# Spreading three batches' transform stages over a gated FFN, with a first stage in three products

## The chip, the cores and the metric

The kernel runs on one core of a Trainium2 chip. The metric is the device time of one execution in microseconds (us), the median of several runs. Engines are named as in the profile: PE (TensorE matmul), PEld (its weight loads), DVE (VectorE), ACT (ScalarE), POOL (GpSimd), SP (SyncE, which here issues nearly all DMAs, in order).

## The reference

For `x` of 8 batches x 3136 positions x 256 channels: a real FFT along the positions, a product with a complex filter, the inverse FFT, and then a gated feed-forward network whose gate is a three-tap convolution along the positions:

```
X = rfft(x, axis=1);  y = irfft(X * (filt_r + 1j * filt_i), n=3136, axis=1)
h = maximum(y @ w_in, 0)                       # 256 -> 1024
conv[s] = sum_k conv_w[k] * h[s + k - 1]       # per channel, zeros outside the batch
out = (h * sigmoid(conv)) @ w_out              # 1024 -> 256
```

## The kernel before, in words

**The transform of a batch** is four stages of matmuls, each in 14 operations of two columns ("pairs", q = 0 to 13). 3136 = 112 x 28. Stage "1" multiplies 112 rows of x by a table of its own for every column (`s1`), stage "2" does the 28-point transforms, then DVE multiplies by the filter in three instructions and POOL adds (`filt`), stage "3" goes back, and stage "4" multiplies by another table for every column (`m2`) and leaves y, which is kept in SBUF as two fp32r parts, a rounded one and the rest. Between "1" and "2", and between "3" and "4", the data go through DRAM (`a_dram`, `r_dram`, `b_dram`), because rows and columns change places. So "2" of a batch can load only when its "1" is stored completely, and "4" when its "3" is (`ready`).

A float32 matmul costs PE more than an fp32r one. Where accuracy asks for it, `mm3` replaces one float32 product by three fp32r products of parts (rounded x rounded, rounded x rest, rest x rounded). The FFN's matmuls (lines 187 to 189 under the name `ps_h`, and 586 to 588) are of this kind, and so is stage "2" from batch 2 on: stage "1" stores both parts (`store_first`). Stages "1" (line 275), "3" (line 279) and "4" (line 313) are plain float32.

**The FFN** runs in units of 510 positions, each with 8 blocks of 128 hidden channels. One unit and block is one *step* m; there are 400. A step's work is pipelined over seven steps: `inner(m)` (the matmuls into `ps_h`, 3 PSUM banks), then relu and the taps on ACT and DVE, sigmoid, gate, the split into `g` parts (ACT rounds, POOL subtracts), and six steps later `project`, which adds to `po`. At the last block of a unit (every step with m = 6 modulo 8), DVE copies `po` out (`evacuate`, line 599) and SP stores it (lines 604 and 617).

**The order around the change** is written out by hand, and every engine and SP keep it. Batch 0's transform runs ahead of the loop. From then on the transforms of batches 1 to 7 are placed into steps: `plan[m]` lists the operations of step m. With NW = 48 steps a batch, window t holds stages "2", "3" and "4" of batch t and stage "1" of batch t + 1: "2" at steps 2 to 25 of the window (9 steps for 5 operations), "3" three steps behind it, "4" at steps 33 to 44 (more than one a step), and "1" in the steps with least other work. In each step come, in this order: `evacuate`; `from_bank` for the operations of the step before (PSUM bank `ps_t` to SBUF, stores); `want_in` (loads); `transform` for the new operations, at the head of PE's step; `inner`; the FFN's other parts; `project`.

`want_in` loads the inputs in the order of the plan, at most 6 ahead. It stops at the first one whose stage is not stored yet, or whose buffers are all out: three `tia` for stage "2" (two loads each, line 244), three `tin` for "1" and "4" (line 253). `want_table` loads the tables of "1" and "4" (line 678; three operations ahead, four `tab` buffers), `want_filter` the filter of the next "2" (line 683, two buffers). PSUM has three `ps_t` banks.

Where a unit reaches into the next batch, `join_tail` and `join_head` copy the tail of one y and the head of the next into a tile `yx`.

Of the kernel before, what the change touches and what calls it, by code (L numbers as in the profile page):

```python
# [17 lines left out]
N1 = 112  # L18
# [18 lines left out]
def _dft_tables():  # L37
# [78 lines left out]
    tall[:N1] = s1  # L116
    return {"s1": tall, "s2": s2(False), "s2s": s2(True), "one": np.eye(128), "s3": s3(False), "s3s": s3(True), "m2": m2, "m2g": turned}

# [14 lines left out]
def tile_fft_filter_gated_ffn(  # L133
# [7 lines left out]
    w_out: bass.AP,  # L141
    s1: bass.AP,
    s2: bass.AP,
    s2s: bass.AP,
# [67 lines left out]
    wo = [wc.tile([128, NF, D], F32R, name=f"wo{h}") for h in range(2)]  # L212
    turned = [wc.tile([120, 2, D], F32, name=f"v{k}") for k in range(2)]
    for v in turned:
# [21 lines left out]
    def load_in(pool, kind, b, q):  # L236
        if kind == "2" and b == 1:
            r = pool.tile([112, 2, 2, D], F32R, name="tia", bufs=3)[:, 0].bitcast(F32)
            nc.sync.dma_start(out=r, in_=a_in[b][:, pair(q)])
            return r  # L240
        if kind == "2":
            r = pool.tile([112, 2, 2, D], F32R, name="tia", bufs=3)
            for h, t in enumerate((a_in, r_in)):
                nc.sync.dma_start(out=r[:, h].bitcast(F32), in_=t[b][:, pair(q)])
            return r
        if kind == "1" and b == 1:
            if q % 2 == 0:
                t = pool.tile([128, 2, 2, D], F32, name="filt")
                nc.sync.dma_start(out=t.rearrange("p a j d -> p (a j) d"), in_=xt[N1:N1 + 128, 2 * q:2 * q + 4])
                fours.append(t)  # L250
            return fours[-1][0:112, q % 2]
        r = pool.tile([128, 2, D], F32, name="tin", bufs=3)[0:112]
        nc.sync.dma_start(out=r, in_={"1": xv, "4": b_in}[kind][b][:, pair(q)])
        return r
# [18 lines left out]
    def by_column(ps, w, r):  # L273
        for j in range(2):
            nc.tensor.matmul(ps[0:112, j * D:j * D + D], lhsT=w[:, j], rhs=r[:, j], start=True, stop=True)  # L275

    def by_row(o, q, r, m, ms):
# [20 lines left out]
    def filt(ps, q, f):  # L298

        pp, v = ps[0:120].rearrange("p (j d) -> p j d", d=D), turned[q % 2]  # L300
        z = tp.tile([128, 2, D], F32, name="z", bufs=3)[0:120]
        nc.vector.tensor_mul(z, pp, f[0:120, :, 0])
        nc.vector.tensor_mul(v[64:120], pp[0:56], f[0:56, :, 1])
        nc.vector.scalar_tensor_tensor(out=v[0:56], in0=pp[64:120], scalar=-1.0, in1=f[64:120, :, 1], op0=ALU.mult, op1=ALU.mult)  # L304
        nc.gpsimd.tensor_tensor(out=z, in0=z, in1=v, op=ALU.add)  # L305
        return z
# [13 lines left out]
    raws = {}  # L320
    conv_raw = tp.tile([128, 1, 6 * NF], I32, name="conv_raw", bufs=1)

    def load_weights(k, pool):
        if pool is tp:
            raws[k] = [pool.tile([128, 2, 2, D], F32R, name="tia", bufs=3).rearrange("p a j d -> p a (j d)").bitcast(I32) for _ in range(2)]
# [14 lines left out]
    def convert(k, pool):  # L340

        for j in range(2):
            if pool is tp:
                if j == 0:
                    em = pool.tile([128, 2, 2, D], F32R, name="tia", bufs=3).bitcast(I32)
                w, raw = pool.tile([128, 2, D], F32, name="z", bufs=3), raws[k][j]
# [14 lines left out]
    with (  # L361
# [39 lines left out]
        with tc.tile_pool(name="sq", bufs=2) as sq:  # L401
# [43 lines left out]
            for i in range(NP + 4):  # L445
# [18 lines left out]
                if i == 5:  # L464
                    table("1", 0)
                    for q in range(AHEAD):
                        r = tp.tile([128, 2, D], F32, name="tin", bufs=3)
                        nc.sync.dma_start(out=r, in_=xt[N1:N1 + 128, pair(q)])
# [8 lines left out]
        for q in range(NP + 1):  # L477
# [3 lines left out]
            if q:  # L481
# [141 lines left out]
    def put(m, kind, b, q):  # L623
        plan.setdefault(m, []).append((kind, b, q))

    for t in range(1, B):
        w = NW * (t - 1)
        used = [0] * NW
        if t == 1:
            at1 = [q // 2 for q in range(NP - AHEAD)]  # L630
            at2, at4 = [9 + 3 * q // 2 for q in range(NP)], [35 + 10 * q // NP for q in range(NP)]
            for q, s in enumerate(at1):
                put(s, "1", 1, AHEAD + q)
                used[s] += 1
        else:
            at2, at4 = [2 + 9 * q // 5 for q in range(NP)], [33 + 12 * q // NP for q in range(NP)]
        for q in range(NP):
            for s, kind, cost in ((at2[q], "2", 3), (at2[q] + 3, "3", 1), (at4[q], "4", 1)):
                put(w + s, kind, t, q)
                used[s] += cost  # L640
        if t + 1 < B:
            spots = []
            for q in range(NP):
                s = min(range(5 if t == 1 else 0, NW - 2), key=lambda s: (used[s], s))
                used[s] += 2
                spots.append(s)
            for q, s in enumerate(sorted(spots)):
                put(w + s, "1", t + 1, q)
        tails[w + 29] = heads[w + 46] = next(u for u in range(NU) if joins(u) and place(u)[0] == t - 1)
        assert NF * tails[w + 29] >= w + NW  # L650
    order = [(m, op) for m in sorted(plan) for op in plan[m]]
    inputs = [op for _, op in order if op[0] in "124"]
    tables = [op for _, op in order if op[0] in "14"]
    filters = [op for _, op in order if op[0] == "2"]
# [4 lines left out]
    def ready(op):  # L659
        kind, b, _ = op  # L660
        return kind == "1" or stored.get(({"2": "1", "4": "3"}[kind], b), 0) == NP

# [11 lines left out]
    def want_table(n):  # L674
        for op in tables[n:n + 1]:
            src = {"1": s1, "4": m2}[op[0]]
            got_table[op] = t = tp.tile([112, 2, 112], F32, name="tab", bufs=4)
            nc.sync.dma_start(out=t, in_=src[0:112, pair(op[2])])

# [4 lines left out]

    done, wanted = {"in": 0, "table": 0, "filter": 0}, {"in": 0}
    def transform(op):
        kind, b, q = op
        banks[op] = ps = ps_t.tile([128, 512], F32, name="ps_t")
        if kind in "124":
            done["in"] += 1  # L690
            r = got_in.pop(op)
        if kind in "14":
            want_table(done["table"] + 3)
            done["table"] += 1
            w = got_table.pop(op)
        if kind == "1":
            by_column(ps, w, r)
        if kind == "2":
# [5 lines left out]
        if kind == "4":  # L704
            fourth(ps, r, w)

    def from_bank(op):
# [11 lines left out]
        if kind == "4":  # L719
            vs[op] = v = tp.tile([128, 2, D], F32, name="z", bufs=3).rearrange("p j d -> p (j d)")[:, 0:4 * N1]  # L720
            nc.vector.tensor_copy(v, ps[:, 0:4 * N1])
# [10 lines left out]
    with tc.manual_schedule(engines=COMPUTE | {mybir.EngineType.SP}):  # L732
        want_in()
        for n in range(3):
            want_table(n)
        late = convert(3, tp)
        for m in range(NF * NU + PLAG + 1):
            p1, p2, p3, p4, p6, p7 = (at(m - k) for k in (1, 2, 3, 4, PLAG, PLAG + 1))
            new, old = plan.get(m, []), plan.get(m - 1, [])
            if p7:  # L740
# [83 lines left out]
```

## Time and profile before

| | |
|---|---|
| median of 3 runs (lowest, highest) | 1540.9 us (1539.38, 1542.57) |
| the profiled execution: time, span | 1538.35 us, 1536.5 us |
| granted TensorE clock, mean | 0.997 |
| stage "1" of batches 2 to 7: 336 instructions (four to an operation) | 86.3 us of busy time |
| DMA: bytes moved, mean rate | 268.46 MB, 175 GB/s |
| DMA queue of SP: share of 16 engines' span | 58.0% |

Rows of groups read: line, engine, operation, what it writes <- reads, shape, how often | busy us in total, mean ns of one | idle time before them and who ended it. A matmul's mean is its latency; matmuls overlap, so the cost of one to PE is the distance to the next. Rows of the timeline read: start, duration, engine, line, operation; those of the chain: start, duration, what. Rows of waits: who waited <- for whom: us in total, times, longest.

### The profile page before, as it was taken

To read this page: it belongs to the slowest core of one execution; us is meant where nothing else is said; L and a number is where in the kernel's file an instruction comes from. 1 tells how busy PE (TensorE), PEld (TensorE's weight loads), DVE (VectorE), ACT (ScalarE), POOL (GpSimd) and SP (SyncE) were. 2 spreads that over 40 slices of the span, in tenths; PEclk is the share of its full clock that TensorE was granted. 3 is DMA by queue.
4 is the path that set the end of the run, shared out by engine and by line. 5 is a ranking of instruction groups with operands and counts; after the bars stand their busy time and mean duration, and the time that the engine had idled before them with its cause. 6 is when DMAs were issued, how large, how long until landed. Compare 5 with 4: busy or idle time off the path is not lost.

```text
span 1536.5 us, 26897 instructions
## 1 busy us (share of the span) xinstructions
PE 1506.2 (98%) x9292; PEld 1305.2 (85%) x9292; DVE 1235.6 (80%) x1894; ACT 1143.7 (74%) x1973; POOL 830.8 (54%) x725
## 2 busy tenths in 40 slices
PE   6989999999999999999999999999999999999999
PEld 5867789888898889988898888988899888989998
DVE  7988886888778887788878987788877888777776
ACT  3576678766787777876788667876688667888886
POOL 4635456554574455645565455745556455754443
PEclk9999999999999999999999999999999999999999
DMA  8768764787539755597546885388554763300001
GB/s 301 246 180 241 233 202 136 222 251 210 170 117 275 233 172 179 154 268 228 176 137 203 238 241 170 109 252 256 171 173 117 207 182 99 106 29 15 28 28 31
DMA packets 188967, 268.46 MB, mean 175 GB/s; under 512 B 19056, under 2 KB 130528, under 8 KB 188832
## 3 DMA queue, kind: packets, MB, share of 16 engines
q1 hardware_dynamic: 188352, 266.29, 58.0%
q8 instruction: 74, 1.21, 0.3%
q14 instruction: 61, 0.50, 0.1%
q10 hardware_dynamic: 480, 0.46, 0.1%
HBM read 176.76 MB, written 89.92 MB: 174 GB/s over the span
## 4 chain that ended last, share of the span: by engine, by line
PE 88%; DVE 4%; issue 3%; DMA 2%; POOL 2%; ACT 1%; SPq 0%; POOLq 0%; ACTq 0%; DVEq 0%
PE ps_h L187 11%; PE ps_h L189 11%; PE ps_h L188 11%; PE po L586 11%; PE po L588 11%; PE po L587 11%; PE ps_t L313 6%; PE ps_t L279 5%; PE ps_t L275 5%; PE ps_t L187 1%; PE ps_t L188 1%; PE ps_t L189 1%; POOL g L162 1%; DMA tin<-b_dram 1%; PE ps L386 1%
## 5 line engine op out<-in xcount | busy, mean ns | idle before, releaser
L554 DVE SCALAR_TENSOR_TENSOR t<-ps_h,cw,t 128x510 f32<-128x510 f32 (+1 forms) x800 | 588.6, 736 | 247.3 <-ACT t L550 243.7
L162 POOL TENSOR_TENSOR g<-t,g 128x510 fp32r<-128x510 f32 (+1 forms) x400 | 506.2, 1275 | 200.4 <-ACT g L156 186.7
L586 PE MATMUL po<-wo,g 128*128 128x256 f32 (+1 forms) x1576 | 439.6, 279 | 0.1
L588 PE MATMUL po<-wo,g 128*128 128x256 f32 (+1 forms) x1576 | 439.1, 279 | 0.0
L587 PE MATMUL po<-wo,g 128*128 128x256 f32 (+1 forms) x1576 | 438.6, 278 | 0.0
L550 ACT ACTIVATE t<-ps_h,cw 128x510 f32<-128x510 f32 (+1 forms) x400 | 272.7, 682 | 151.4 <-POOL g L162 122.0
L545 ACT ACTIVATE ps_h<-ps_h 128x512 f32<-128x512 f32 (+1 forms) x400 | 235.2, 588 | 178.5 <-PE ps_h L189 176.1
L305 POOL TENSOR_TENSOR z<-z,v 120x512 f32<-120x512 f32 x112 | 145.5, 1299 | 356.6 <-DVE v L304 291.1
L187 PE MATMUL ps_h<-y,wi 128*128 128x512 f32 (+1 forms) x688 | 311.5, 453 | 2.9 <-DVE t L560 1.7
L586 PEld LDWEIGHTS po<-wo,g 128*128 128x128 f32 (+1 forms) x1576 | 296.7, 188 | 17.1 <-ACT g L156 0.3
L587 PEld LDWEIGHTS po<-wo,g 128*128 128x128 f32 (+1 forms) x1576 | 296.1, 188 | 17.2
L588 PEld LDWEIGHTS po<-wo,g 128*128 128x128 f32 (+1 forms) x1576 | 296.6, 188 | 0.5 <-POOL g L162 0.4
L189 PE MATMUL ps_h<-y,wi 128*128 128x512 f32 (+1 forms) x688 | 269.8, 392 | 0.3 <-POOL wi L162 0.3
L188 PE MATMUL ps_h<-y,wi 128*128 128x512 f32 (+1 forms) x688 | 269.6, 392 | 0.0
L560 DVE TENSOR_TENSOR t<-ps_h,t 128x510 f32<-128x510 f32 (+1 forms) x400 | 268.6, 672 | 1.1 <-ACT t L557 0.8
L557 ACT ACTIVATE t<-t 128x510 f32<-128x510 f32 (+1 forms) x400 | 245.5, 614 | 3.0 <-DVE t L554 2.9
L156 ACT ACTIVATE g<-t 128x510 fp32r<-128x510 f32 (+1 forms) x400 | 245.1, 613 | 0.2 <-DVE t L560 0.2
L162 POOL TENSOR_TENSOR y<-z,y 128x448 fp32r<-128x448 f32 x98 | 138.4, 1422 | 98.7 <-ACT y L156 94.8
L187 PEld LDWEIGHTS ps_h<-y,wi 128*128 128x128 f32 x688 | 129.9, 189 | 39.8 <-DVE t L560 7.8
L189 PEld LDWEIGHTS ps_h<-y,wi 128*128 128x128 f32 x688 | 129.8, 189 | 30.6 <-POOL wi L162 0.7
L188 PEld LDWEIGHTS ps_h<-y,wi 128*128 128x128 f32 x688 | 130.4, 189 | 29.8 <-issue 10.9
L313 PE MATMUL ps_t<-tab,tin 112*128 112x112 f32 x784 | 102.0, 274 | 3.9 <-DMA tin<-b_dram 2.0
(124 smaller groups left out, 1718.4 us busy)
## 6 DMA issues: line engine op xcount, KB each, us to landing
filt<-in_filt SPq DMA_DIRECT2D x98, 512.0 KB
tia<-a_dram SPq DMA_DIRECT2D x98, 224.0 KB
b_dram<-st SPq DMA_DIRECT2D x98, 224.0 KB
tin<-b_dram SPq DMA_DIRECT2D x98, 224.0 KB
a_dram<-sh SPq DMA_DIRECT2D x90, 224.0 KB
tin<-in_x SPq DMA_DIRECT2D x84, 224.0 KB
r_dram<-sh SPq DMA_DIRECT2D x84, 224.0 KB
tia<-r_dram SPq DMA_DIRECT2D x84, 224.0 KB
```

What stands on the lines that cost most here:

```text
L156: nc.scalar.activation(dst, src, AF.Copy)
L162: nc.gpsimd.tensor_tensor(out=dst, in0=src, in1=hi.bitcast(F32), op=ALU.subtract)
L187: nc.tensor.matmul(ps, lhsT=wh, rhs=rh, start=start, stop=False, **kw)
L188: nc.tensor.matmul(ps, lhsT=wh, rhs=rl, start=False, stop=False, **kw)
L189: nc.tensor.matmul(ps, lhsT=wl, rhs=rh, start=False, stop=stop, **kw)
L550: nc.scalar.activation(t, hs[u, f][:, 1:n + 1], AF.Copy, scale=cw[:, 1, f:f + 1])
L554: nc.vector.scalar_tensor_tensor(out=t, in0=h[:, k:place(u)[2] + k], scalar=cw[:, k, f:f + 1], in1=t, op0=ALU.mult, op1=ALU.add)
L557: nc.scalar.activation(ts[u, f], ts[u, f], AF.Sigmoid)
L560: nc.vector.tensor_mul(ts[u, f], hs.pop((u, f))[:, 1:place(u)[2] + 1], ts[u, f])
L586: nc.tensor.matmul(o, lhsT=gh[:, c:c + n], rhs=wo[0][:, f], start=first, stop=False, skip_group_check=True)
L587: nc.tensor.matmul(o, lhsT=gh[:, c:c + n], rhs=wo[1][:, f], start=False, stop=False, skip_group_check=True)
L588: nc.tensor.matmul(o, lhsT=gl[:, c:c + n], rhs=wo[0][:, f], start=False, stop=last, skip_group_check=True)
```

## The change

Stage "1" from batch 2 on is made of three fp32r products. Its table comes as two parts, made on the host (`s1p`) and copied by seven DMAs into a DRAM tile of its own (`s1_dram`) while batch 0's stage "4" runs; each operation loads two `tab` tiles, one for each column. The parts of x are made by POOL in a new operation "0", which stands two steps ahead of its "1": a cast and a subtraction into a tile `parts`.

The plan is new. Stages are spread by hand-given ranges (`at1`, `at2`, `at4`) over more steps, so that up to three batches are under way in one window, and `settle` moves an operation on until its step has no more than one other. The buffers change: `tia` 3 to 2, `tin` 3 to 4, `tab` 4 to 5, `z` 3 to 4, `parts` 2 new. `yx`, the late weight conversion's scratch and `conv_raw` use tiles of `parts` and `z` instead of their own, and `join_tail` moves from step 29 to step 44 of a window. In the new plan, stages "2" to "4" of batches 2 to 7 stand in these steps: "2" 50-71, 85-108, 123-150, 166-193, 207-238, 241-278; "3" three steps later; "4" 76-92, 115-140, 158-187, 201-235, 244-283, 289-330. Stage "1" stands in 10-38, 58-80, 83-119, 122-162, 165-203, 206-232.

```diff
+    parts[:, :, 0] = ((whole.view(np.uint32) + np.uint32(0x800)) & np.uint32(0xFFFFF000)).view(np.float32)
+    parts[:, :, 1] = whole - parts[:, :, 0]
...
+    s1_dram = dram.tile([N1, N2, 2, 112], F32, name="s1_dram")
...
-            r = pool.tile([112, 2, 2, D], F32R, name="tia", bufs=3)
+            r = pool.tile([112, 2, 2, D], F32R, name="tia", bufs=2)
...
-        r = pool.tile([128, 2, D], F32, name="tin", bufs=3)[0:112]
-        nc.sync.dma_start(out=r, in_={"1": xv, "4": b_in}[kind][b][:, pair(q)])
+        r = pool.tile([128, 2, D], F32, name="tin", bufs=4)[0:112]
+        nc.sync.dma_start(out=r, in_={"0": xv, "4": b_in}[kind][b][:, pair(q)])
...
+    def split_in(pool, x):
+        parts = pool.tile([128, 2, 2, D], F32R, name="parts", bufs=2)[0:112]
+
+        def make():
+            nc.gpsimd.tensor_copy(parts[:, 0], x)
+            lo_pool(parts[:, 1], x, parts[:, 0])
+
+        return parts, make
+
+    def by_column_split(ps, ws, r):
+        for j, w in enumerate(ws):
+            mm3(ps[0:112, j * D:j * D + D], w[:, 0], w[:, 1], r[:, 0, j], r[:, 1, j])
...
             steps(early, 1)
+            if q < 7:
+                nc.sync.dma_start(out=s1_dram[:, 4 * q:4 * q + 4], in_=s1p[:, 4 * q:4 * q + 4])
...
-        joined[u] = [wp.tile([128, KT, UO + 2], F32R, name=f"yx{h}", bufs=1) for h in range(2)]
+        joined[u] = [wp.tile([128, 2, 2, D], F32R, name="parts", bufs=2).rearrange("p a j d -> p a (j d)") for _ in range(2)]
...
+    at1 = {2: [(0, 10, 41)], 3: [(1, 10, 34)], 4: [(1, 35, 43), (2, 10, 25)], 5: [(2, 26, 43), (3, 10, 20)], 6: [(3, 21, 43), (4, 10, 13)], 7: [(4, 14, 43)]}
+    at2 = {1: (9, 30), 2: (50, 71), 3: (84, 110), 4: (123, 153), 5: (166, 196), 6: (207, 239), 7: (240, 281)}
+    at4 = {1: (35, 45), 2: (76, 94), 3: (115, 142), 4: (158, 190), 5: (201, 238), 6: (244, 286), 7: (289, 334)}
+    count = [0] * (NW * B)
+
+    def settle(s, *later):
+        while max(count[s + d] for d in (0, *later)) >= 2:
+            s += 1
+        for d in (0, *later):
+            count[s + d] += 1
+        return s
+
+    def spread(steps):
+        return [steps[q * len(steps) // NP] for q in range(NP)]
+
+    for q in range(AHEAD, NP):
+        put(settle((q - AHEAD) // 2), "1", 1, q)
+    for b in range(2, B):
+        for q, m in enumerate(spread([NW * i + s for i, lo, hi in at1[b] for s in range(lo, hi)])):
+            m = settle(m)
+            assert 10 <= m % NW <= 43
+            put(m - 2, "0", b, q)
+            put(m, "1", b, q)
+    for b in range(1, B):
+        for q, m in enumerate(spread(range(*at4[b]))):
+            put(settle(m), "4", b, q)
+        for q, m in enumerate(spread(range(*at2[b]))):
+            m = settle(m, 3)
+            put(m, "2", b, q)
+            put(m + 3, "3", b, q)
     for t in range(1, B):
         w = NW * (t - 1)
...
-        tails[w + 29] = heads[w + 46] = next(u for u in range(NU) if joins(u) and place(u)[0] == t - 1)
+        tails[w + 44] = heads[w + 46] = next(u for u in range(NU) if joins(u) and place(u)[0] == t - 1)
...
     def want_in():
         while wanted["in"] < min(done["in"] + 6, len(inputs)) and ready(inputs[wanted["in"]]):
             op = inputs[wanted["in"]]
-            if sum(place_of(o) == place_of(op) for o in got_in) == (4 if place_of(op) == "x" else 3):
+            if sum(place_of(o) == place_of(op) for o in got_in) == {"x": 4, True: 2, False: 4}[place_of(op)]:
                 break
...
+        for key in tables[wanted["table"]:n]:
+            kind, b, i = key
+            t = tp.tile([112, 2, 112], F32R, name="tab", bufs=5)
+            src = s1_dram[:, i] if kind == "1" and b > 1 else {"1": s1, "4": m2}[kind][0:112, pair(i)]
+            nc.sync.dma_start(out=t.bitcast(F32), in_=src)
...
+    def tables_for(op):
+        keys = tables_of(op)
+        want_table(tables.index(keys[-1]) + 4)
+        return [got_table.pop(key) for key in keys]
...
-            later = [to_y(op) for op in old]
+            later = [to_y(op) for op in old] + [split(op) for op in plan.get(m, []) if op[0] == "0"]
```

More of the change, by code (lines that the diff above doesn't have):

```diff
@@ L212, in tile_fft_filter_gated_ffn @@
     wo = [wc.tile([128, NF, D], F32R, name=f"wo{h}") for h in range(2)]
-    turned = [wc.tile([120, 2, D], F32, name=f"v{k}") for k in range(2)]
+    turned = [wc.tile([120, 2 * D + 8], F32, name=f"v{k}")[:, 0:2 * D].rearrange("p (j d) -> p j d", d=D) for k in range(2)]
     for v in turned:
@@ L320, in tile_fft_filter_gated_ffn @@
     raws = {}
-    conv_raw = tp.tile([128, 1, 6 * NF], I32, name="conv_raw", bufs=1)
+    conv_raw = tp.tile([128, 1, 2 * D], F32, name="z", bufs=4).bitcast(I32)[:, :, 0:6 * NF]
     def load_weights(k, pool):
         if pool is tp:
-            raws[k] = [pool.tile([128, 2, 2, D], F32R, name="tia", bufs=3).rearrange("p a j d -> p a (j d)").bitcast(I32) for _ in range(2)]
+            raws[k] = [pool.tile([128, 2, 2, D], F32R, name="tia", bufs=2).rearrange("p a j d -> p a (j d)").bitcast(I32) for _ in range(2)]
             for j in range(2):
@@ L344, in convert @@
                 if j == 0:
-                    em = pool.tile([128, 2, 2, D], F32R, name="tia", bufs=3).bitcast(I32)
-                w, raw = pool.tile([128, 2, D], F32, name="z", bufs=3), raws[k][j]
+                    em = wp.tile([128, 2, 2, D], F32R, name="parts", bufs=2).bitcast(I32)
+                w, raw = pool.tile([128, 2, D], F32, name="z", bufs=4), raws[k][j]
             else:
@@ L626, in tile_fft_filter_gated_ffn @@
     for t in range(1, B):
         w = NW * (t - 1)
[L628 to L640, printed above, removed]
@@ L651, in tile_fft_filter_gated_ffn, with tables_of @@
+        assert NF * tails[w + 44] >= w + NW
+    when = {op: m for m in plan for op in plan[m]}
+    for b in range(2, B):
+        assert when["1", b, NP - 1] + 1 < when["2", b, 0] and when["3", b, NP - 1] + 1 < when["4", b, 0] and when["4", b, NP - 1] <= NW * b - 3
+    def tables_of(op):
+        kind, b, q = op
+        return [(kind, b, 2 * q + j) for j in range(2)] if kind == "1" and b > 1 else [op] if kind in "14" else []
     order = [(m, op) for m in sorted(plan) for op in plan[m]]
-    inputs = [op for _, op in order if op[0] in "124"]
@@ L653, in tile_fft_filter_gated_ffn @@
-    tables = [op for _, op in order if op[0] in "14"]
+    inputs = [op for _, op in order if op[0] in "024" or op[0:2] == ("1", 1)]
+    tables = [key for _, op in order for key in tables_of(op)]
     filters = [op for _, op in order if op[0] == "2"]
@@ L660, in ready @@
         kind, b, _ = op
-        return kind == "1" or stored.get(({"2": "1", "4": "3"}[kind], b), 0) == NP
+        return kind in "01" or stored.get(({"2": "1", "4": "3"}[kind], b), 0) == NP
     def place_of(op):
@@ L674, in want_table @@
     def want_table(n):
[L675 to L678, printed above, removed]
+        for key in tables[wanted["table"]:n]:
[3 more added lines that the diff above has]
+            nc.sync.dma_start(out=t.bitcast(F32), in_=src)
+            got_table[key] = t
+            wanted["table"] += 1
+    def tables_for(op):
+        keys = tables_of(op)
+        want_table(tables.index(keys[-1]) + 4)
+        return [got_table.pop(key) for key in keys]
     def want_filter(n):
@@ L683, in want_filter, with split @@
             nc.sync.dma_start(out=f, in_=filt_in[:, pair(op[2])])
-    done, wanted = {"in": 0, "table": 0, "filter": 0}, {"in": 0}
+    done, wanted = {"in": 0, "filter": 0}, {"in": 0, "table": 0}
+    parts = {}
+    def split(op):
+        done["in"] += 1
+        parts[op[1:]], low = split_in(wp, got_in.pop(op))
+        return low
     def transform(op):
@@ L692, in transform @@
         if kind in "14":
[L693 to L697, printed above, removed]
+            w = tables_for(op)
+        if kind == "1" and b == 1:
+            by_column(ps, w[0].bitcast(F32), r)
+        if kind == "1" and b > 1:
+            by_column_split(ps, w, parts.pop((b, q)))
         if kind == "2":
@@ L704, in transform @@
         if kind == "4":
-            fourth(ps, r, w)
+            fourth(ps, r, w[0].bitcast(F32))
     def from_bank(op):
@@ L733, in tile_fft_filter_gated_ffn @@
         want_in()
-        for n in range(3):
-            want_table(n)
+        want_table(3)
         late = convert(3, tp)
@@ L738, in tile_fft_filter_gated_ffn @@
             p1, p2, p3, p4, p6, p7 = (at(m - k) for k in (1, 2, 3, 4, PLAG, PLAG + 1))
-            new, old = plan.get(m, []), plan.get(m - 1, [])
+            new, old = ([op for op in plan.get(i, []) if op[0] != "0"] for i in (m, m - 1))
             if p7:
```

24 lines of the change are left out of this document (9 added, 15 removed).

## The prediction

> **What bounds the kernel now.** I read the page first, then the windows by stage, then the chain in order of time, then the queue of SP.
>
> ```profile
> span 1536.5 us, 26897 instructions
> PE 1506.2 (98%) x9292; PEld 1305.2 (85%) x9292; DVE 1235.6 (80%) x1894; ACT 1143.7 (74%) x1973; POOL 830.8 (54%) x725
> PE 88%; DVE 4%; issue 3%; DMA 2%; POOL 2%; ACT 1%; SPq 0%; POOLq 0%; ACTq 0%; DVEq 0%
> ```
>
> The chain that ended last is 88% PE. A busy PE alone says little, since matmuls overlap, so the windows must show that nothing else holds it:
>
> ```profile
> 70.00:80.00 10.00, 10.00 (x89) 9.80 (x88) 9.94 (x12) 9.93 (x15) 5.26 (x11) 1.00 0.29 81
> 88.00:115.00 27.00, 20.58 (x85) 14.94 (x85) 20.02 (x32) 18.74 (x33) 9.08 (x11) 1.00 0.84 247
> 620.00:800.00 180.00, 179.24 (x1097) 155.69 (x1096) 147.55 (x226) 136.20 (x234) 98.83 (x83) 1.00 0.67 199
> ```
>
> Columns: window, length, then busy time of PE, weight loads, DVE, ACT, POOL, granted clock, DMA share, GB/s. In a steady batch (620 to 800) PE misses 0.8 us of 180; DVE has 32 us to spare, POOL 81. So only two things move the time: shorter PE work, and new moments at which PE waits. PE runs its queue in order, so a wait of a "transform" at the head of a step delays everything behind it and is not won back.
>
> **The change, part by part.**
>
> *First stage as three products.* 84 operations (batches 2 to 7) are rewritten.
>
> ```profile
> L275 PE MATMUL ps_t<-tin,tab 112*112 112x256 f32 x336 | 86.3, 378 | 0.0
> 634.38 0.87 PE ps_t L275 x4
> 376.89 0.28 PE L187 MATMUL ps_t<-tia,s 112*120 112x256 f32 x1
> ...
> 377.49 0.28 PE L189 MATMUL ps_t<-tia,s2s 112*120 112x256 f32 x1
> 377.61 0.39 PE L187 MATMUL ps_h<-y,wi 128*128 128x512 f32 x1
> ```
>
> 336 instructions are four for each of 84; on the chain one operation takes 0.87 us. The second stage's last pair already is what the first becomes: six fp32r products of 256 columns with 112 rows. They start at 376.89 and the next matmul at 377.61: 0.72 us. Gain 84 x 0.15 = 12.6 us; with 0.86 for the old one 11.8. I take 12.6. Six weights are loaded in place of four; in these rows the loads hide behind products 0.12 us apart.
>
> The Trainium skill ("FP8 and Floating Point Precision", TensorE Precision Notes) says that true FP32 makes four passes through the array; three products of one pass would then take 3/4 of 0.87, 0.65 us, and the gain would be 18 us. The rows above give 0.72, a ratio of 0.83, so the sum goes by the rows.
>
> *POOL makes the parts.* 84 casts and 84 subtractions of 112x512.
>
> ```profile
> L162 POOL TENSOR_TENSOR g<-t,g 128x510 fp32r<-128x510 f32 x392 | 502.9, 1292 | 192.5 <-ACT g L156 181.3 <-PE ps_h L189 5.1 <-POOL g L162 3.8
> L532 POOL CAST yx<-y 128x560 fp32r<-128x560 f32 x1 | 0.7, 650 | 0.1
> 700.21 0.75 DVE L554 SCALAR_TENSOR_TENSOR t<-ps_h,cw,t 128x510 f32<-128x510 f32 x1
> 703.04 1.31 POOL L305 TENSOR_TENSOR z<-z,v 120x512 f32<-120x512 f32 x1 [4.28 <-DVE v L304]
> 704.25 0.74 DVE L554 SCALAR_TENSOR_TENSOR t<-ps_h,cw,t 128x510 f32<-128x510 f32 x1
> 704.29 2.54 POOL L162 TENSOR_TENSOR g<-t,g 128x510 fp32r<-128x510 f32 x2
> ```
>
> 1.29 + 0.6 = 1.9 us each, 160 us in all: POOL goes from 54% to 65%. The split is two steps ahead of its product, which covers it: zero on the path. Does more POOL slow DVE? At 700.21 POOL was idle, at 704.25 it worked throughout: 0.75 and 0.74 us. Zero. The Trainium skill ("GPSIMD Engine Reference", Key points) warns of contention where DVE reads two SBUF inputs; once the weights are converted, the DVE instructions of the main loop read PSUM for one of theirs, which agrees.
>
> *Copy of the table, twice the tables.* Seven DRAM copies of 401 KB (2.8 MB) are issued beside the fourth stage of batch 0. The DMA engines are 29% busy there, at 81 GB/s in 70 to 80 (row above); at the 247 GB/s of the row below it the copies need 11 us of them. Hidden: 0. Were that cover gone they would push into 88 to 115, where PE misses 6.4 us already: up to +3. One more 98 KB table per operation: 84 issues on SP, at 0.3 to 0.4 us each (as in the SP rows below), beside PE.
>
> *Spreading.* DVE was not the limit, so thinning its load gains nothing by itself. It takes away the runs of fourth-stage operations whose inputs came one step ahead:
>
> ```profile
> L313 PE MATMUL ps_t<-tab,tin 112*128 112x112 f32 x784 | 102.0, 274 | 3.9 <-DMA tin<-b_dram 2.0 <-issue 1.0 <-DVE t L554 0.6
> 242.65 0.41 SPq L604 DMA_DIRECT2D out<-ot  x1
> 243.33 0.85 SPq L617 DMA_DIRECT2D out<-ot  x2
> 244.24 0.88 SPq L253 DMA_DIRECT2D tin<-b_dram  x2
> 247.35 1.12 PE L313 MATMUL ps_t<-tab,tin 112*128 112x112 f32 x8 [1.12 <-DMA tin<-b_dram]
> 425.32 1.37 DVE L599 COPY ot<-po 128x512 f32<-128x512 f32 x2 [0.96 <-PE po L588]
> 426.04 0.40 SPq L604 DMA_DIRECT2D out<-ot  x1
> 426.61 0.48 PE L187 MATMUL ps_h<-y,wi 128*128 128x512 f32 x1
> 426.72 0.84 SPq L617 DMA_DIRECT2D out<-ot  x2
> 427.68 0.34 SPq L253 DMA_DIRECT2D tin<-b_dram  x1
> 430.67 1.12 PE L313 MATMUL ps_t<-tab,tin 112*128 112x112 f32 x8 [0.16 <-DMA tin<-b_dram]
> 603.55 0.88 PE ps_t L313 x8
> 661.66 0.86 PE ps_t L279 x2
> ```
>
> These rows are the yardstick for the rest. Every eighth step (m = 6 modulo 8) a unit is evacuated, and SP, in order, waits for DVE's two copies before its stores and everything behind them. Step 86 began at 425.73 (one fourth-stage operation, 0.88, ahead of the inner matmul at 426.61). The copies ended at 0.96 us after that, the stores at 1.83, the load behind them at 2.29, and PE used it 2.65 us after that. So a load issued in an evacuation step for the next one is late: 1.12 us of idle PE at 247. Removed: L313's idle time, -4 us (0 to -6).
>
> What replaces it I get by walking the new plan through "want_in" and "want_table", step by step, with the new limits (two "tia", four "tin", five "tab"):
>
> (a) Step 238. Second-stage operations 11 and 12 of batch 6 both stand in step 237 and hold both "tia" buffers, so the load for operation 13 is issued only in step 238, which uses it. Ahead of it on SP stand the filter load for 13, whose buffer DVE frees after its three multiplies for operation 11, which stand behind the two evacuation copies, and then the stores.
>
> ```profile
> L302 DVE TENSOR_TENSOR z<-ps_t,filt 120x512 f32<-120x512 f32 x98 | 66.9, 683 | 2.6 <-DMA filt<-in_filt 1.5 <-PE po L588 0.9
> L303 DVE TENSOR_TENSOR v<-ps_t,filt 56x512 f32<-56x512 f32 x98 | 67.0, 684 | 1.4
> L304 DVE SCALAR_TENSOR_TENSOR v<-ps_t,filt 56x512 f32<-56x512 f32 x98 | 67.9, 693 | 1.4
> L159 DVE TENSOR_TENSOR sh<-ps_t,sh 112x512 fp32r<-112x512 f32 x84 | 57.4, 683 | 3.4 <-ACT sh L156 3.3
> SPq L683 <- DVE v L304: 61.2, 26, 5.1
> ```
>
> From the step's start: copies 0.96, multiplies 2.06, filter issue 0.4, stores 1.5, two loads 0.9, landing 2.65: 8.5 us. PE would have come to it after one third-stage operation, at 0.86. +7.6 us. Without the filter's wait 4.5; with 1.5 MB queued at once 9.
>
> (b) Evacuation steps 14, 38, 70, 78, 86, 94 issue a load or a table for the next step (before: seven such, the ones above). By the yardstick 0.3 to 1.7 us each: +5 (2 to 8).
>
> (c) Three PSUM banks "ps_t": in steps 22, 38, 86, 126, 134, 174, 182 an operation needs the bank of one of the step before, which DVE frees (0.68 us, L159) behind the evacuation copies: at 1.64 where PE comes at 0.7 to 0.88. 7 x 0.7, and steps 38 and 86 stand in (b) already: +4 (0 to 6). The old trace has no such case; its evacuation steps reused banks that ACT frees.
>
> (d) Pairs of second-stage operations in steps 19, 231 and 233 put filter waits ahead of the next loads: +2 (0 to 4). (e) The third stage of batch 2 ends in step 74 and the fourth begins in 76 (before: four or five steps later): store, wait, load fit by a hair, +0.5 (0 to 3). (f) Moving the tail copy from step 29 to 44 leaves it four steps of cover: 0.
>
> Sum: -12.6 - 4 + 7.6 + 5 + 4 + 2 + 0.5 = +2.5 us on the profiled execution, which took 1538.35 us (span 1536.5), 2.5 below the median of 1540.9. Waits in neighbouring steps partly share their time, since after one the queues have caught up; I take 1.5 off and forecast +1: 1542 us on the median's scale. About 0.2% (3.1 us) is what a measurement can tell from no change, so the forecast is no change.
>
> **The rivals.**
>
> *Faster, 1533.* The waits of (b) to (e) are mostly absorbed, as the same kind was before: seven late loads cost only 3.9 us together. Then -12.6 - 4 + 7.6 + 1 = -8. If step 238 is covered too, 1526. For it: PE's gain is certain to about 1 us. Against it: step 238 follows from order alone.
>
> *Slower, 1552.* One mechanism: "tin" buffers are now freed by POOL's split at the end of a step instead of by PE at its head. Where four are out, SP waits for that split before it issues the next load, and the tables behind it, of which 41 now come one step ahead (before: 7), come late. POOL's split ends up to 1.5 us into the next step when a z addition (1.3 us, L305 above) and a g subtraction (1.29) stand ahead of it; SP then issues at about 2.9, and landing makes it some 5.5 against a step of 4.4. At 1 us for ten of these it is +10. It decides from about four on. For it: DVE's steps lag most where second and first stages meet (steps 56 to 71, 85 to 108). Against: most splits stand in steps without a z addition.
>
> *The three products take 3/4 of the old time.* Gain 18 instead of 12.6 with the waits as summed: 1536. This needs 0.108 us for a product where the row gives 0.12.
>
> *The products do not run at that price* (112 weight columns instead of 120): each 0.02 us is 10 us, 1552. Nothing in the rows speaks for it.
>
> **How the numbers follow.** No change 0.38. Faster 0.32 (absorbed waits 0.28, 3/4 0.04). Slower 0.30 (POOL holding SP, or (b) and (c) at their upper ends, 0.28; dear products 0.02). The likeliest's own range is 1538 to 1544, the bound on either side of 1540.9. For 8 in 10 I reach into both other cases: 1530 to 1552.
>
> **What would show it.** Right: operations of the first stage at 0.72 us on the chain; DVE durations unchanged; one PE wait of 5 to 9 us on "tia" three fifths through, just after an evacuation; a handful of waits of about 1 us on DMA or DVE behind evacuation copies; L313's idle below 2 us. Wrong: if total idle before PE's "ps_t" matmuls in the main loop is below 10 us, the waits were absorbed and it is faster; if waits on "tab" are many and SP's waits name POOL, it is slower.

## The result, and the profile after

| | before | changed |
|---|---|---|
| median (lowest, highest) | 1540.6 us (1539.38, 1542.57) | 1607.1 us (1606.42, 1609.3) |
| ratio, 95% interval | | 1.0433 [1.0415, 1.0451] |
| profiled span, mean granted clock | 1536.5 us, 0.997 | 1606.0 us, 0.981 |

The change makes the kernel 66 us slower; the forecast was no change. Page of the changed kernel (busy times; chain by engine, then by line):

```profile
span 1606.0 us, 27532 instructions
PE 1520.9 (95%) x9460; PEld 1322.7 (82%) x9460; DVE 1237.6 (77%) x1894; ACT 1143.7 (71%) x1973; POOL 984.4 (61%) x893
PE 73%; DMA 6%; POOL 6%; DVE 6%; issue 5%; ACT 3%; SPq 1%; POOLq 0%; ACTq 0%; DVEq 0%
```

PE's share of the chain falls from 88% to 73%, and no other engine has taken its place: DMA, POOL, DVE and issue each hold some 6%. So there is no new bound but many places where PE stands. The windows show where. Columns as in the prediction: window, length, busy time of PE, weight loads, DVE, ACT, POOL, granted clock, DMA share, GB/s. First the kernel before, then the changed one:

```profile
440.00:800.00 360.00, 359.03 (x2196) 312.00 (x2195) 293.92 (x451) 272.90 (x466) 197.67 (x165) 1.00 0.67 199
```

```profile
116.00:440.00 324.00, 299.61 (x1782) 251.65 (x1783) 243.37 (x372) 215.15 (x373) 210.07 (x195) 0.97 0.71 208
440.00:800.00 360.00, 339.05 (x2098) 295.82 (x2097) 275.86 (x423) 253.49 (x433) 243.56 (x219) 0.98 0.72 212
800.00:1160.00 360.00, 344.44 (x2112) 297.31 (x2111) 281.59 (x431) 253.30 (x433) 239.44 (x212) 0.98 0.75 218
1160.00:1500.00 340.00, 339.56 (x2204) 304.68 (x2204) 265.63 (x406) 277.49 (x472) 189.17 (x153) 1.00 0.24 72
```

PE misses 24, 21 and 16 us in the first three windows and 0.4 in the last, where no first stages are left. Where it misses time the clock is lower too. What it waited for (waits of PE, then of its weight loads; in total, times, longest), and the view of the tile `tab`:

```profile
PE ps_t L192 <- DMA tab<-s_dram: 27.6, 11, 6.3
PE ps_t L192 <- DMA tia<-a_dram: 11.2, 2, 8.4
PE ps_t L332 <- DMA tab<-in_m: 5.0, 5, 1.5
PEld ps_t L192 <- DMA tab<-s_dram: 22.7, 10, 6.6
```

```profile
  DMA tab<-s_dram: 50.3, 21
```

The new tables of parts (`s_dram`) come late eleven times, 27.6 us of idle PE. The 21 waits of the view count most of them twice, since PE's weight loads wait for the same tables. One of them, in the timelines of SP and then of PE:

```profile
349.94 3.20 SPq L638 DMA_DIRECT2D out<-ot  x7
353.23 0.34 SPq L269 DMA_DIRECT2D a_dram<-sh  x1
353.67 0.40 SPq L272 DMA_DIRECT2D r_dram<-sh  x1
354.17 0.45 SPq L250 DMA_DIRECT2D tia<-a_dram  x1
...
357.06 1.55 SPq L718 DMA_DIRECT2D tab<-s_dram  x2
```

```profile
358.00 0.28 PE L194 MATMUL ps_t<-parts,tab 112*112 112x256 f32 x1
364.62 0.55 PE L192 MATMUL ps_t<-parts,tab 112*112 112x256 f32 x1 [6.34 <-DMA tab<-s_dram]
367.53 0.63 PE L193 MATMUL ps_h<-y,wi 128*128 128x512 f32 x1
367.96 0.63 PE L194 MATMUL ps_h<-y,wi 128*128 128x512 f32 x1
```

After an evacuation SP issues for 8 us on end, and the tables stand last. Between 353.23 and 357.06 it issues two stores, four second-stage loads, one first-stage load and a filter. By the sizes on the page of the changed kernel (the stores and the first-stage load are 224 KB each as well),

```profile
filt<-in_filt SPq DMA_DIRECT2D x98, 512.0 KB
tia<-a_dram SPq DMA_DIRECT2D x98, 224.0 KB
```

that is 7 x 224 + 512 = 2080 KB issued just ahead of the tables. The windows around the wait:

```profile
358.00:364.00 6.00, 0.28 (x2) 0.06 (x1) 3.86 (x7) 2.75 (x6) 5.92 (x6) 0.68 1.00 276
364.00:368.00 4.00, 3.38 (x8) 2.12 (x9) 0.69 (x1) 1.19 (x2) 0.54 (x1) 0.50 0.58 176
```

The DMA engines are full (1.00, 276 GB/s) while PE stands. By the trace's DMA packets, 1466 of the 2080 KB were still to be moved at 357.06. They, 200 KB of the tables and 378 KB of stores that were issued behind the tables make 2045 KB, which took 7.4 us at 281 GB/s. The first packet of a table starts only at 360.8, and the pair's last ones end at about 364.4. Then a second price shows: from 364 to 368 the granted clock is 0.50, and the matmuls into `ps_h`, 0.23 us apart otherwise, come 0.43 us apart (367.53, 367.96).

From the starts of all matmuls I split the time of PE's main loop in the profiled span: waits (gaps of over 0.25 us beyond the median distance of a shape) went from 10.5 to 72.4 us, the extra time of matmuls at half clock from 0 to 19.4, and the work itself fell by 13.3. With 1.5 us before the loop that is 69.5, the difference of the spans.

### The profile page after: what moved, and what is told of

The parts are those of the page before. It is cut to its first block, busy times and chain, and to the rows that moved or that the text cites. A ratio compares the mean times of both kernels' runs of the same rounds, so it can differ in the third digit from the quotient of the medians.

```text
span 1606.0 us, 27532 instructions
## 1 busy us (share of the span) xinstructions
PE 1520.9 (95%) x9460; PEld 1322.7 (82%) x9460; DVE 1237.6 (77%) x1894; ACT 1143.7 (71%) x1973; POOL 984.4 (61%) x893
## 4 chain that ended last, share of the span: by engine, by line
PE 73%; DMA 6%; POOL 6%; DVE 6%; issue 5%; ACT 3%; SPq 1%; POOLq 0%; ACTq 0%; DVEq 0%
PE ps_h L192 10%; PE ps_h L194 10%; PE ps_h L193 10%; PE po L607 9%; PE po L608 9%; PE po L609 9%; PE ps_t L332 5%; PE ps_t L298 4%; DMA tab<-s_dram 3%; POOL g L167 2%; PE ps_t L192 2%; PE ps_t L193 2%; PE ps_t L194 2%; DMA tab<-in_m 1%; POOL parts L167 1%
## 5 line engine op out<-in xcount | busy, mean ns | idle before, releaser
L192 PEld LDWEIGHTS ps_h<-y,wi 128*128 128x128 f32 x688 | 132.5, 193 | 39.7 <-issue 11.8
L193 PEld LDWEIGHTS ps_h<-y,wi 128*128 128x128 f32 x688 | 133.1, 193 | 32.2 <-issue 13.8
L194 PEld LDWEIGHTS ps_h<-y,wi 128*128 128x128 f32 x688 | 132.4, 192 | 31.6 <-POOL wi L167 0.7
L167 POOL TENSOR_TENSOR parts<-tin,parts 112x512 fp32r<-112x512 f32 x84 | 108.6, 1292 | 6.7
```

The lines of the kernel that those rows point to most:

```text
L167: nc.gpsimd.tensor_tensor(out=dst, in0=src, in1=hi.bitcast(F32), op=ALU.subtract)
L192: nc.tensor.matmul(ps, lhsT=wh, rhs=rh, start=start, stop=False, **kw)
L193: nc.tensor.matmul(ps, lhsT=wh, rhs=rl, start=False, stop=False, **kw)
L194: nc.tensor.matmul(ps, lhsT=wl, rhs=rh, start=False, stop=stop, **kw)
```

## The experiments

Waits and half clock are those of the split just described, in the main loop of the profiled span. Ratios are to the kernel before on the same chip.

| kernel | median, us | ratio [95%] | waits | half clock |
|---|---|---|---|---|
| before | 1540.6 | | 10.5 | 0 |
| changed | 1607.1 | 1.0433 [1.0415, 1.0451] | 72.4 | 19.4 |
| e3 plan alone, f32 first stage | 1572.0 | 1.0209 [1.0190, 1.0228] | 36.3 | 5.6 |
| e1 no table loads | 1560.5 | 1.0140 [1.0125, 1.0155] | 38.6 | 10.1 |
| e2 tables ahead of the outputs | 1582.3 | 1.0274 [1.0241, 1.0307] | 51.3 | 12.9 |
| e6 seven table buffers, two tables more ahead | 1580.8 | 1.0290 [1.0267, 1.0312] | 49.2 | 9.9 |
| e12 both | 1572.1 | 1.0208 [1.0193, 1.0223] | 45.2 | 10.8 |
| e4 batch 5's fourth stage earlier | 1604.3 | 1.0432 [1.0415, 1.0450] | 69.8 | 13.2 |
| e13 e12 with the edit of e4 | 1559.9 | 1.0138 [1.0120, 1.0156] | 34.3 | 6.0 |
| e5 e3 with the old buffers | 1586.5 | 1.0313 [1.0293, 1.0333] | 40.6 | 10.0 |
| e9 e5 with the tables' size kept | 1580.1 | 1.0265 [1.0243, 1.0287] | 40.7 | 9.1 |
| e7 changed, three `tia`, three `tin` | 1613.4 | 1.0497 [1.0465, 1.0528] | 78.8 | 25.7 |
| e10 before, 128 bytes further | 1547.4 | 1.0048 [1.0033, 1.0063] | 7.9 | 0 |
| e8 products in the old spacing | 1538.5 | 1.0000 [0.9984, 1.0015] | 20.1 | 3.7 |
| e11 e8 with seven table buffers | 1523.8 | 0.9894 [0.9879, 0.9909] | 6.1 | 0.9 |

### The change taken apart: e3 and e1

e3 keeps the plan and the buffers, and leaves the first stage in f32 with one table (no parts, no copy to `s1_dram`):

```diff
-            put(m - 2, "0", b, q)
...
-        return [(kind, b, 2 * q + j) for j in range(2)] if kind == "1" and b > 1 else [op] if kind in "14" else []
+        return [op] if kind in "14" else []
...
-            by_column_split(ps, w, parts.pop((b, q)))
```

> The new plan and buffers with the first stage as before: one float32 product per column, one table tile per operation, three operations ahead, no POOL parts, no copy of the table. Theory A: 1540 to 1560 (the 1541 before, plus the wait in step 238 with its slow clock, 8 to 13 us, less or more a few). Theory B: 1580 or more.

e1 keeps everything but the loads of the parts' tables: all first stages from batch 2 on use one table that stays in SBUF, so the values are not the transform's.

```diff
-            w = tables_for(op)
+            w = tables_for(op) if tables_of(op) else [resident, resident]
```

> The first stage of batches 2 to 7 uses one resident table tile for every column instead of loading its two tiles per operation (so its values are not those of the transform). Theory A (tables come too late: the second table of an operation is issued only one operation ahead, behind everything SP holds): the 50 us of PE idle that the changed kernel shows on s1_dram tables go, and with them most of the half-clock stretches that follow long waits: 1530 to 1550. Theory B (the plan itself: three batches side by side with two tia buffers and tin buffers that POOL frees make all loads late; the tables are only the last in line): the waits move to the next load, 1580 to 1605.

The four kernels make a ladder: plan and buffers +33 us (1538.8, before on the same chip, to 1572.0), parts on POOL and three products without table loads -11.5 (to 1560.5), table loads +47 (to 1607.1; 45 by the ratios). Neither e3 nor e1 falls into a range that was expected for it; both lie between the two.

The 11.5 is not the products' price alone. In the profiled spans of e3 and e1, 10.6 us apart, PE's work falls by 12.4 us and the time ahead of the loop by 4.9, while waits and half clock grow by 6.8. The 12.4 is what is to be held against the predicted 12.6. PE's waits that name `parts` come to 0.8 us in e1, and 2.7 on its weight loads, so POOL's 0 nearly holds on PE itself. The tables, priced at 0, are the largest term.

### Why the tables are late: e2, e6, e12

e2 asks for the tables at the start of a step, ahead of the evacuation's stores:

```diff
+            first = next((op for op in new if tables_of(op)), None)
+            if first:
+                want_table(tables.index(tables_of(first)[-1]) + 4)
             if p7:
                 evacuate(*p7)
```

> Nothing is left out; the table loads of a step are issued at the step's start, ahead of the evacuation's stores, the stage stores and the input loads. Theory A: with tables ahead of the burst instead of behind it, most of the 50 us go, 1535 to 1560. Theory B: the tables arrive but the inputs behind them are later by as much, 1585 to 1605. If A holds but the cause is the short lead of one operation and not the place in SP's queue: 1580 to 1600 as well, with waits still on the tables.

In the changed kernel an operation asks for the three tables behind its own two. So the first table of an operation is asked for two operations ahead, and the second only one. e6 asks for two more, so that the second comes two operations ahead, with seven buffers (`z` three, and one buffer fewer for the filters in the time ahead of the loop, which grows by 5.6 us):

```diff
-            t = tp.tile([112, 2, 112], F32R, name="tab", bufs=5)
+            t = tp.tile([112, 2, 112], F32R, name="tab", bufs=7)
...
-        want_table(tables.index(keys[-1]) + 4)
+        want_table(tables.index(keys[-1]) + 6)
```

> The changed kernel with seven tab buffers and tables loaded one whole first-stage operation further ahead (two tables more); paid for by z at three and one buffer less of the filter ahead of the main loop. If the short lead is what makes the tables late: the 47 us that the run without tables gained come back nearly all, 1560 to 1572. If it is their place at the end of SP's bursts: 1590 to 1605.

e12 does both, and keeps the filters' buffers.

> The changed kernel with seven table buffers, tables asked for six ahead and at the start of a step, ahead of the outputs' transfers (three z buffers). Theory 'lateness in one queue': tables wait no more and the outputs, not the inputs, stand behind them: the tables' 47 us nearly go, 1558 to 1568 us, as without table loads (e1). Rival 'the issues themselves': 84 more issues of 1.5 us on SP make the second-stage inputs late wherever the tables stand: 1575 to 1585 us, as e6, with 20 us or more of TensorE behind tia.

Each alone brings 25 or 26 us, both 35 of the 47. With e2, waits on tables of parts are left (8.5 us of PE), as its third case expected; in e6 and e12 none is. Both of these end between the two ranges that were expected for them. (The 1.5 us of e12's rival is what the two issues of a pair took in the burst shown above; the median of one is 0.42 us.) In e6 PE waits more for second-stage inputs than in the changed kernel (11.2), but hardly more than in e1, which loads no such tables. The rows of e6 and of e1:

```profile
PE ps_t L192 <- DMA tia<-a_dram: 16.9, 6, 10.2
```

```profile
PE ps_t L192 <- DMA tia<-a_dram: 14.4, 5, 8.4
```

So a table's lateness is made by its place in the queue and by the lead at which it is asked for, and most of the wait for inputs that e6 shows is the plan's own, which late tables had covered. The remaining 12 us (e12 against e1) were not taken apart; SP's further issues and the 98 KB each are the candidates.

### Step 238: e4 and e13

The fourth stage of batch 5 ends eight steps earlier. By `settle` this moves second and third stages of batch 6 as well: no step holds two of its second-stage operations any more (before: steps 231, 233 and 237), and its last one stands in step 236. One line changes, cut here to the range in question:

```diff
-    at4 = {..., 5: (201, 238), ...}
+    at4 = {..., 5: (201, 230), ...}
```

> Only the range of batch 5's fourth stage is shortened (201 to 230 instead of 201 to 238), so that no two second-stage operations share a step near 237 and none is loaded in the step that uses it. Both theories: the 8.8 us wait at 1102 us goes and with it about 10 us of half clock: 1607 becomes 1590 to 1598. If the wait only moves to a neighbour: 1603 to 1610.

> As e12, with the fourth stage of the sixth batch ending eight steps earlier (steps 201 to 229 in place of 201 to 237), which lets the inputs of the next second stages be asked for in time. In e12 TensorE waits 10.7 us at step 238 and the clock is half for some 10 us after it, about 15 us in all. Theory 'each wait of the plan has its own price': with no late tables left to take its place, the time falls by 10 to 15 us, to 1557 to 1563 us. Rival 'something else is late next': as in e4, where the same edit gave 3 us, another transfer is late in its place and the time stays at 1567 us or more.

The same edit gives 3 us in the changed kernel and 12.2 on top of e12 (10.8 by the ratios, since e13 ran on another chip). The rows of e12, then of e13:

```profile
PE ps_t L192 <- DMA tia<-a_dram: 17.3, 6, 10.3
```

```profile
PE ps_t L192 <- DMA tia<-a_dram: 6.0, 4, 2.1
```

In e4's profiled span the wait at step 238 is gone, but between steps 208 and 229, where the changed kernel has none of over 0.7 us, seven such waits take some 8 us, three of them behind tables and three behind DVE. In e13 three waits of 0.9 to 1.7 us stand there, and the wait of 10.3 us and some of the half clock behind it go for good. So the plan's largest wait has its own price, as long as nothing else is late beside it. The edit also crowds steps 201 to 230, so e4 does not show whether its new waits are the old one moved or come from that.

### Buffers and addresses: e5, e7, e9, e10

e5 gives e3 the old buffers (three `tia`, three `tin`, three `z`, four `tab`), e7 gives the changed kernel three `tia`, `tin` and `z`:

```diff
-            if sum(...) == {"x": 4, True: 2, False: 4}[place_of(op)]:
+            if sum(...) == {"x": 4, True: 3, False: 3}[place_of(op)]:
```

> The new plan with float32 first stage (as in the run of the plan alone, 1572) but with the old buffers: three tia, three tin, four tab, three z. Theory A (of the plan's 33 us some 20 come from the third tia buffer that was given up: a second-stage input is loaded one operation later): 1545 to 1555, the 9 us wait in step 238 gone. Theory B (the placement itself: evacuation steps, PSUM banks, bursts): 1562 to 1572.

> The changed kernel with three tia, three tin and three z buffers instead of two, four and four. Waits on tia (18 us) go with their slow clock: 1580 to 1590. If the tables then take over the same time, or three tin buffers make SP wait more for POOL: 1600 to 1615.

Both are slower than what they start from. Since `tin` and `z` lose a buffer in the same edit, this does not price the third `tia` alone. In e5 the products of the down projection also came further apart. Four `tab` buffers instead of five move everything that is allocated behind them by 896 bytes. e9 is e5 with five, which is also one more buffer for tables; e10 is the kernel before with everything behind `turned` moved:

```diff
-    turned = [wc.tile([120, 2, D], F32, name=f"v{k}") for k in range(2)]
+    turned = [wc.tile([120, 2 * D + 16], F32, name=f"v{k}")[:, 0:2 * D].rearrange("p (j d) -> p j d", d=D) for k in range(2)]
```

> As e3 (the new plan with the first stage in f32, no parts, no tables of parts), but with three buffers of second-stage inputs, three of the other inputs and three of z; the tables keep five buffers, so that everything allocated behind them stays where it is in e3. Theory 'addresses': what made e5 slower than e3 (+14 us) was not the input buffers but the shift of everything behind the tables by 896 bytes, since each product of the down projection came 117 instead of 114 ns after the one before; here it is 114 again and the time that of e3, 1565 to 1575 us. Rival 'buffers': three buffers of the other inputs cost these 14 us; then 1583 to 1590 us with the projection at 114 ns. If three buffers of second-stage inputs were what the plan lacks, below 1560 us.

> The kernel before, each of the two tiles turned longer by 16 floats, so that everything allocated behind them lies 128 bytes further; nothing else differs. Theory 'addresses': the products of the down projection go from 114 to 117 ns, 4704 x 3 ns = 14 us slower, 1550 to 1556 us. Rival: 128 bytes matter to nothing and e5's 117 ns has another source: 1537 to 1542 us at 114 ns.

Both theories of e9 were half right. e5 lost 14.5 us to e3: 6.4 of it go with the fifth table buffer (e9 against e5), 8 with the other buffers (e9 against e3). That the 6.4 are addresses fits the products, 117.4 ns apart in e5 and 115.5 in e9, in the mean of the distances under 130 ns. e10 shows the addresses alone: +7.2 us [5.1, 9.7], half of what was expected. Rows of one step's twelve products, first of the kernel before, then of e10:

```profile
700.48 0.28 PE L586 MATMUL po<-wo,g 128*128 128x256 f32 x1
...
701.74 0.28 PE L588 MATMUL po<-wo,g 128*128 128x256 f32 x1
```

```profile
701.86 0.28 PE L586 MATMUL po<-wo,g 128*128 128x256 f32 x1
...
703.15 0.28 PE L588 MATMUL po<-wo,g 128*128 128x256 f32 x1
```

Eleven distances take 1.26 and 1.29 us, 114.5 and 117.3 ns. I had taken the commonest distances, 114 against 117 ns, for all 4704; but before, many steps stand at 118 as well. The means over all 4320 distances under 130 ns are 115.5 and 117.5 ns, 8.6 us in sum.

e9 against e3 shows something else: with three `tia` PE's 17.7 us behind second-stage inputs shrink to 0.7, and waits on DVE and fourth-stage inputs stand in their place; the waits in sum are 40.7 us against 36.3.

```profile
PE ps_h L192 <- DVE t L578: 5.6, 11, 1.2
PE ps_t L331 <- DMA tin<-b_dram: 4.6, 4, 3.9
PE ps_t L331 <- DVE t L572: 4.5, 4, 2.2
```

### The old spacing: e8 and e11

e8 puts stages "2", "3" and "4" back into the steps of the kernel before and keeps parts and products; "1" goes where least else stands in steps 10 to 43 of each window. It has three `tia`, `tin` and `z`, and asks for tables first:

```diff
+            at2, at4 = [2 + 9 * q // 5 for q in range(NP)], [33 + 12 * q // NP for q in range(NP)]
...
+                s = min(range(10, 44), key=lambda s: (used[s], s))
...
+                put(w + s - 2, "0", t + 1, q)
+                put(w + s, "1", t + 1, q)
```

> The old spacing of stages 2, 3 and 4 (each batch in its own window of 48 steps) with the first stage as three products, its operations in steps 10 to 43 of a window; three tia, three tin, three z, five tab; tables issued at a step's start. If the old spacing has room for the tables: the product's 12 us come through, 1526 to 1540. If two tables for an operation are late in any plan with this lead: 1555 to 1585.

e11 is the same with the seven table buffers and the longer lead of e6, two `tia` and four `tin`. That makes it e12 in all but the plan.

> As e8 (second, third and fourth stages where the kernel before has them, three products of parts from the third batch on), with seven table buffers asked for six tables ahead, two buffers of second-stage inputs and four of the other inputs. Theory 'late tables eat the products' gain': e8's 9 us behind tables and 2 us behind inputs go, the half clock after them too, and the 12 us of the products show: 1524 to 1531 us, no wait of TensorE on a table. Rival 'what is late next': as in e6, the table issues ahead of the other transfers make second-stage inputs late instead: 1534 to 1542 us, waits on tia in place of those on tab.

e8 has next to none of the plan's waits for second-stage inputs, but its waits are 20.1 us against 10.5 in the kernel before, and with 3.7 us of half clock they eat the products' gain. The largest after the loop's start are those on tables, 7.3 us of PE:

```profile
PE ps_t L192 <- DMA tab<-s_dram: 7.3, 7, 2.2
```

e11 loses these and beats both kernels: 16.4 us faster than before. The down projection's products lie as far apart in e11 as before (115.6 and 115.5 ns), so addresses have no part in this. Its page and its one wait on a table:

```profile
span 1522.2 us, 27622 instructions
PE 1494.5 (98%) x9460; PEld 1304.4 (86%) x9460; DVE 1235.5 (81%) x1894; ACT 1138.3 (75%) x1973; POOL 984.6 (65%) x893
PE 90%; DVE 4%; ACT 2%; issue 1%; DMA 1%; POOL 1%; SPq 0%; POOLq 0%; ACTq 0%; DVEq 0%
```

```profile
PE ps_t L192 <- DMA tab<-in_m: 0.8, 1, 0.8
```

The windows of e11 and of e12, whose plan alone differs:

```profile
440.00:800.00 360.00, 360.00 (x2292) 316.05 (x2291) 296.95 (x456) 276.26 (x475) 253.58 (x224) 1.00 0.71 208
800.00:1160.00 360.00, 360.00 (x2298) 315.98 (x2297) 297.52 (x458) 276.13 (x476) 254.19 (x224) 1.00 0.71 208
```

```profile
440.00:800.00 360.00, 353.61 (x2223) 308.51 (x2222) 295.02 (x453) 265.50 (x457) 258.22 (x232) 1.00 0.79 234
800.00:1160.00 360.00, 344.22 (x2115) 296.26 (x2114) 283.61 (x435) 255.78 (x440) 234.19 (x205) 0.98 0.70 207
```

PE misses nothing in e11 and 22 us here in e12. Between the two kernels lie 48 us, by the split 39 of waits and 10 of half clock. The new plan costs that; the parts on POOL, the twofold tables and two `tia` buffers, which e11 has too, do not.

## Why the prediction was wrong

**The three products: right.** 0.15 us for each of 84 was forecast, 12.6 in all; PE's work fell by 13.3 us from before to changed and by 12.4 from e3 to e1. In the changed kernel an operation's first product and the next operation's lie 0.70 us apart where nothing is late:

```profile
638.78 0.28 PE L192 MATMUL ps_t<-parts,tab 112*112 112x256 f32 x1
...
639.48 0.40 PE L192 MATMUL ps_t<-tia,s 112*120 112x512 f32 x1
```

**POOL's split, 0: right for DVE and nearly for PE.** DVE's busy time is 1237.6 us against 1235.6; what the split does through SP stands below, under the rival. **The table's copy, 0:** the time ahead of the loop grew by 1.5 us, within the bound of 3; but it is 88.8, 92.2 and 92.9 us in e5, e9 and e3, which have no copy, against 90.0 in the changed kernel, so no cost of the copy is shown.

**"84 issues on SP ... beside PE": the step that failed, 47 us.** The issue time was about as forecast, but what PE waits for is the landing of what is issued last. The prediction's sum has no wait for the tables; they measure +47 us (e1 to the changed kernel). A lead that was three operations is one operation for the second of two tables, often one step, and `want_table` stands behind outputs, stores and inputs in one queue. The yardstick was wrong with it: 2.65 us from the end of the issue to the use came from a step with one 224 KB load behind the stores. With 1466 KB still to be moved ahead of the tables it was 6.0 us from the end of the two issues (358.61) and 7.6 from their start. A landing time read from one row holds for the bytes that stood ahead of that row.

**(a) Step 238: right in place and about right for the wait, low in price.** +7.6 was forecast. The rows of SP and PE:

```profile
1095.07 0.35 SPq L730 DMA_DIRECT2D filt<-in_filt  x1
1095.47 0.43 SPq L625 DMA_DIRECT2D out<-ot  x1
1095.94 0.98 SPq L638 DMA_DIRECT2D out<-ot  x2
1097.02 0.41 SPq L250 DMA_DIRECT2D tia<-a_dram  x1
1097.47 0.71 SPq L250 DMA_DIRECT2D tia<-r_dram  x1
```

```profile
1101.54 0.54 PE L192 MATMUL ps_t<-tia,s 112*120 112x256 f32 x1 [8.37 <-DMA tia<-a_dram]
```

Filter, stores, two loads: the order of the prediction, 8.4 us of idle PE, and then half clock, which the prediction left out. The edit that takes it away gave 12.2 us in e13, with the pairs of steps 231 and 233 gone too.

**(b) to (e): many steps right, the sum low.** In e3, which has no tables of parts, PE waits 0.7 to 2.6 us at steps 15, 22, 38, 86, 95, 126, 134 and 233, which follow from the lists of (b) to (d), and 0.8 to 1.9 us at 21, 31, 40, 67, 88 and 189 among others, which do not. The net of the old wait removed and the new ones was forecast as +15 (19.1 less 4 and before the 1.5 taken off: 7.6 + 5 + 4 + 2 + 0.5 - 4 = 15.1); e3 measures +25.8 of waits and +5.6 of half clock. The discount of 1.5 us for neighbouring waits is small beside that. Its reason is not refuted: in e9 the waits for second-stage inputs go and the sum of the waits does not fall. Why the waits outside the lists stand where they do was not worked out.

**L313's 4 us: not gained.** The fourth stage (now L332) is idle 7.8 us, 5.0 of them for its own tables, which are asked for in one order with the first stage's.

**The half clock: not in the sum at all, 19 us.** Its rows are in the first section, and what it depends on in the last.

**The rival "slower".** It named late tables, and its test (many waits on `tab`, SP's waits naming POOL) came out. Its mechanism has a part in the time. One case, where SP waits from 618.8 to 623.65; rows of POOL, SP (twice) and PE:

```profile
622.33 1.29 POOL L167 TENSOR_TENSOR parts<-tin,parts 112x512 fp32r<-112x512 f32 x1
```

```profile
623.65 0.32 SPq L259 DMA_DIRECT2D tin<-in_x  x1
```

```profile
624.95 0.90 SPq L718 DMA_DIRECT2D tab<-s_dram  x2
```

```profile
629.29 0.34 PE L192 MATMUL ps_t<-parts,tab 112*112 112x256 f32 x1 [3.94 <-DMA tab<-s_dram]
```

The split ends at 623.62, SP's load follows at once, the tables stand behind it, and PE stands for 3.9 us. The late tables of PE's eleven waits (27.6 us) can be followed back in SP's queue to the start of the burst that issued them. Six bursts (12.0 us of PE's waits) start when POOL's split ends, after SP waited 1.3 to 4.7 us for it; three (9.5 us) start at DVE's evacuation copies, as the burst shown further up; two (6.1 us) at another wait. So the rival's price, ten waits of 1 us, is near what its mechanism has a part in; it left out the other bursts and the half clock.

That SP waits for POOL makes nothing late by itself, though. SP's waits, in the changed kernel and in e11:

```profile
SPq L259 <- POOL parts L167: 54.5, 33, 4.7
```

```profile
SPq L259 <- POOL parts L167: 34.6, 31, 2.7
```

In e1, which loads none of these tables, the wait is 59.3 us at 1560 us; in e6, whose tables have a longer lead, 51.1 us, and no table is late. No run took this wait away alone.

## What to carry to other kernels

Price a load by its place in the queue: how many bytes are still to be moved ahead of it when it is issued, at the rate the DMA engines then reach, and how many steps remain until its use. When one operation comes to need two tiles of a kind, a lead counted in tiles shrinks to half or less in operations; raise it with them. Before spreading work evenly, walk every load's issue and use through the new order: e11 shows that a lighter PE pays where the old order of loads is kept, and e12 that the same work in the new order costs 48 us more.

## What the runs showed of the hardware

**A wait of PE is followed by half clock.** In the fifteen profiles, each of 33 gaps in the main loop that were 3 us or more longer than usual was overlapped by a stretch at clock 0.50 or followed by one within 2 us. So were 29 of 41 gaps of 2 to 3 us, and 17 of 168 between 0.8 and 2 us. The stretches last 3.4, 6.8, 10.2 or 13.7 us. The Trainium skill ("TensorE: Matmul & The Clock Gate", Part 1: The HAM clock gate) says that the clock drops to half after an idle window of about 3.4 us of a free-running monitor and comes back after one busy window. The multiples of 3.4 us agree; that 29 of 41 gaps of only 2 to 3 us were enough does not, if the window has to be idle from end to end. In the changed kernel the half clock took 19.4 of 1606 us, 1.2%.

**Where tiles lie costs PE time.** 128 bytes further for everything behind `turned` made the down projection's products come 2.0 ns further apart in the mean and the kernel 7.2 us slower (e10), with nothing else changed. Which of the operands does it, and which addresses are the good ones, was not tried.
